# A spectral layer and a gated product on one core: the sequence transform split 64 x 32 instead of 32 x 64, real and imaginary parts stacked on partitions

## The chip, the cores and the metric

One core of one Trainium2 chip. The time is device microseconds (us) of one execution of the program, and "time" below is the median over executions; the profile is of one further execution. Engines are named as the profile names them: PE (TensorE; PEld are its weight loads), DVE (VectorE), ACT (ScalarE), POOL (GpSimd), SP (the queue that issues nearly all DMAs).

## What is computed

```python
def reference(A_x, A_w_r, A_w_i, B_x, B_w_gate, B_w_up, B_w_down):
    # x: [1, 2048, 640]; w_r, w_i: [2048, 321]; w_gate, w_up: [640, 1536]; w_down: [1536, 640]; all bf16
    xn = _layernorm(A_x, axis=-1)
    X = rfft2(xn, axes=(-2, -1))              # 2048 x 321, complex
    a = irfft2(X * (w_r + 1j * w_i), s=(2048, 640)).astype(bf16)
    b = ((xn @ w_gate) * (xn @ w_up)) @ w_down
    return A_x + a + b
```

## The kernel before

Rows of x are laid out as row = 16 p + j over 128 partitions p. After the layer norm the work has two branches that share every engine.

- The gated product: gate/up matmuls write PSUM (`GU`, narrow blocks of rows at L989, blocks of 512 rows at L969), `copy_on` evicts them (L719 when ACT does it, L720 when DVE does), `H` multiplies (L1005, L1006), and at the end 12 matmuls per output piece (`ACC`, L1229) sum over w_down; one more (`IV`, L1239) adds the spectral branch into the same bank, `FIN` (L1249) adds x and the piece is stored.
- The spectral branch: S1 to S5 (L883 to L917, DVE) do the small factors of the transform along the 640 columns; `R` (L930) the short part of the transform along the 2048 rows; then 16 steps t, each `D` (L1034, the 64-point part along columns), its eviction `eD`, `C` (L1055 to L1058, the long part along rows, a complex product with a real table), `WM` (L1070, L1073: the product with the filter w_r, w_i, four real products kept in fp32), `CD` (L1084, L1086, DVE) and `CB` (L1093, L1094, POOL), which combine the four products into a real and an imaginary part, `NG` (L1101 to L1103, ACT: negated or plain copies for the second operand), `IA` (L1117, L1118, the way back along rows) and its eviction `eIA`; then `I` (L1146) and V1 to V5 (L1170 to L1203, DVE).

The 2048 rows are split as 32 x 64 (`_R = 32`, `_S1 = 64`): R transforms over 32, C over 64, and one step holds one of 16 groups of 128 rows. The imaginary part lies beside the real one in the free dimension, so a complex product of C is four matmuls of 321 columns with three tables (cos, -sin, sin).

No loop order is written by hand. Every piece above is a task with the engines that may run it, a cost in ns (`_d_mm`, `_d_act`, ...), a priority and what it reads and writes. `_Sched.plan` plays the tasks through, choosing for each engine the task to start next, within `slack` of the most urgent one; `caps` bounds how many PSUM units a class of tasks may hold. The result is a fixed order of instructions on each engine, with semaphore waits between engines. A matmul task names a `bank`; the evicting task `frees` it.

Filters come by 64 DMAs (`ld_w`, L713), four a step, of 64 rows of 642 bytes each, into four slots; a slot is loaded again when the `WM` that read it is done. SP's queue is served in order, and it holds the loads of w_down too, which overwrite the inverse tables (`TI`) that IA reads.

The lines around C:

```python
a_r = v_a[:, ar, 0:_LP]
a_i = v_a[:, ar, 324:324 + _LP]
c.e.matmul(ps[:, bk, 0:_LP], v_tf[:, t, 0, :], a_r, start=True, stop=False)
c.e.matmul(ps[:, bk + 1, 0:_LP], v_tf[:, t, 0, :], a_i, start=True, stop=False)
c.e.matmul(ps[:, bk, 0:_LP], v_tf[:, t, 1, :], a_i, start=False, stop=True)
return c.e.matmul(ps[:, bk + 1, 0:_LP], v_tf[:, t, 2, :], a_r, start=False, stop=True)
```

Of the kernel before, what the change touches and what calls it, by code (L numbers as in the profile page):

```python
# [20 lines left out]
class _Task(object):  # L21
# [4 lines left out]
    def __init__(self, tid, name, engs, dur, emit, prio):  # L26
# [10 lines left out]
        self.frees = None  # L37
# [34 lines left out]
class _Sched(object):  # L72
# [55 lines left out]
    def task(self, name, engs, dur, emit, reads=(), writes=(), prio=0.0, after=(), bank=None, frees=None,  # L128
# [7 lines left out]
        t.frees = frees  # L136
        if selffree:
            t.freers.append(t)
        if frees is not None:
            frees.freers.append(t)  # L140
            t.deps.add(frees)
# [13 lines left out]
    def plan(self, nbanks=8, filler_deadline=0.0):  # L155
# [56 lines left out]
        while nsch < ntot:  # L212
# [107 lines left out]
            if t.frees is not None:  # L320
                p = t.frees
                pending_free[p.tid] -= 1
                fe = free_end.get(p.tid, 0.0)
                if t.end > fe:
                    free_end[p.tid] = t.end
                if pending_free[p.tid] == 0:
                    release(p)
# [58 lines left out]
_R = 32  # L386
_S1 = _S // _R
_RR = _S1 // 16
_G = 64 // _S1

# [8 lines left out]
def _build_tables():  # L399
# [56 lines left out]
    a = np.arange(16)[:, None, None, None]  # L456
    r = np.arange(_RR)[None, None, None, :]
    s1 = np.broadcast_to(a + 16 * r, (16, _G, 2, _RR)).reshape(128)
    mg = np.broadcast_to(np.arange(_G)[None, :, None, None], (16, _G, 2, _RR)).reshape(128)
    mck = np.broadcast_to(np.arange(2)[None, None, :, None], (16, _G, 2, _RR)).reshape(128)  # L460
    ng = np.repeat(np.arange(_G), 2 * _S1)
    npm = np.tile(np.repeat(np.arange(2), _S1), _G)
    nk1 = np.tile(np.arange(_S1), 2 * _G)
    tf = np.zeros((128, 16, 3, 128), np.float64)
    ti = np.zeros((128, 16, 2, 128), np.float64)
    for tt in range(16):
        k = _rows(tt, ng, npm, nk1)
        ph = two_pi * ((s1[:, None] * k[None, :]) % _S) / _S
        c = np.exp(-1j * ph)
        same = (mg[:, None] == ng[None, :]).astype(np.float64)  # L470
        ck = np.broadcast_to(mck[:, None], (128, 128))
        pm = np.broadcast_to(npm[None, :], (128, 128))
        f = np.where(ck == 1, np.where(pm == 1, -1j, 1j), 1.0 + 0j)
        i = f
        if tt == 0:
            own = (ck == pm).astype(np.float64)
            z0 = (ng[None, :] == 0)
            f = np.where(z0, own, f)
            i = np.where(z0, own, i)
        fm = c * f * same  # L480
        im = np.conj(c) * i * same / _S
        tf[:, tt, 0] = fm.real
        tf[:, tt, 1] = -fm.imag
        tf[:, tt, 2] = fm.imag
        ti[:, tt, 0] = im.real.T
        ti[:, tt, 1] = im.imag.T
# [5 lines left out]
def _rows(tt, g, pm, k1):  # L492
    q = tt * _G + g
# [15 lines left out]
_NW = 4  # L509
# [3 lines left out]
_YS = 1024  # L513
# [39 lines left out]
def _build(nc, A_x, A_w_r, A_w_i, B_w_gate, B_w_up, B_w_down, out, opts=None):  # L553
# [3 lines left out]
    with es:  # L557
# [8 lines left out]
        sch.caps = {"glu": opts.get("cap_glu", 2), "acc": opts.get("cap_acc", 4), "fill": 1}  # L566
        sch.caps["a"] = opts.get("cap_a", 2)
# [32 lines left out]
        b_w = alloc("W", _NW * 2 * 322)  # L600
        b_tf = alloc("TF", 16 * 3 * 128)
# [10 lines left out]
        b_p = alloc("P", 3 * 4 * 2 * _LP)  # L612
        b_y = alloc("Y", 2 * _YS)
        b_y3 = alloc("Y3", _YS, at=lay["STAT"][0])
# [24 lines left out]
        v_u = V("U").rearrange("p (j t a m) -> p j t a m", j=5, t=16, a=16)  # L639
# [3 lines left out]
        v_w = V("W").rearrange("p (r w l) -> p r w l", r=_NW, w=2)  # L643
# [4 lines left out]
        v_tf = V("TF").rearrange("p (t m k) -> p t m k", t=16, m=3)  # L648
        v_ti = V("TI").rearrange("p (t c n) -> p t c n", t=16, c=2)
# [14 lines left out]
        v_p = V("P").bitcast(_F32).rearrange("p (r w c l) -> p r w c l", r=3, w=2, c=2)  # L664
        v_y = [V("Y")[:, 0:_YS], V("Y")[:, _YS:2 * _YS], V("Y3")]
# [23 lines left out]
        b_wp = sch.buf("wp", 10 ** 9 + 500, 1)  # L689
# [35 lines left out]
        for q in range(4):  # L725
            dma("ld_tf%d" % q, v_tf[:, 4 * q:4 * q + 4], d_tf[:, 4 * q:4 * q + 4],
                128 * 4 * 768, [(b_tf, ("t", 4 * q, 4 * q + 4))], prio=0.31 + 0.01 * q)
# [4 lines left out]
        T("warm_zero", "dve", 150.0, em_wz, writes=[(b_dum, None)], prio=-1.0)  # L732
        for fi in range(opts.get("nfill", 70)):
            def em_fill(c):
                bk = bank_of(c.t)
                c.e.matmul(ps[:, bk, 0:128], v_dum[:, 0:128], v_dum[:, 128:256], start=True, stop=True)
                return c.e.matmul(ps[:, bk, 128:256], v_dum[:, 0:128], v_dum[:, 128:256], start=True,
                                  stop=True)
            T("fill%d" % fi, "pe", 2 * _d_mm(128), em_fill, prio=90.0 + 0.001 * fi, bank="single", cls="fill",
              selffree=True, reads=[(b_dum, None)])  # L740
        nwarm = opts.get("nwarm", 12)
# [8 lines left out]
        T("warm", "pe", opts.get("warm_ns", 5050.0), em_warm, reads=[(b_dum, None)], prio=-1.0,  # L750
          bank="pair", cls="warm", selffree=True)

        def em_wpad(c):
            return c.e.memset(v_w[:, :, :, 321:322], 0.0)
        wpad = T("w_pad", "dve", 80.0, em_wpad, writes=[(b_wp, None)], prio=3.0)


# [3 lines left out]
        muls = {}  # L761
        for gi, (b0, nb) in enumerate(_LN_GROUPS):
            pbase = 1.0 + 0.05 * gi if gi < 4 else opts.get("ln_prio", 5.99) + 0.05 * (gi - opts.get("ln_lead", 4))
            for b in range(b0, b0 + nb):
                if b >= opts.get("act_stats", 6):
# [577 lines left out]
```

## Time and profile before

| | |
|---|---|
| median of 13 runs | 207.05 us (206.52 to 208.01) |
| the profiled execution | 207.06 us, span of its instructions 205.3 us |
| granted TensorE clock | 1.00 |
| HBM read, written | 16.82 MB, 2.62 MB |
| instructions | 4513 |

In a line of groups the columns are: source line, engine, operation, output<-input with sizes, count; then busy us and mean ns of one; then idle time of the engine before them and what ended it. The mean of one is its length from start to end; successive ones overlap on every engine, so what one costs in a row is the distance from start to start, read from a stretch of several. In the chain of waits a line is start us, length us, and the engine (or DMA) and line that the end of the program was waiting for. In the stretches, "(x526)" is a count of instructions. A line of code that is a helper's (L719, L720, L713) gathers all that the helper did.

### The profile page before, as it was taken

The numbers are of one execution on the slowest core, as the hardware profiler recorded it, in microseconds if no ns is written. First come the engines' busy times: TensorE is split into PE (matmuls) and PEld (weight loads), VectorE is DVE, ScalarE is ACT, GpSimd is POOL, SyncE is SP. The second block draws the span as 40 slices with busy tenths as digits, with TensorE's granted clock in tenths as the row PEclk, the third lists the DMA queues.
The fourth block names the chain that finished last, engine by engine and source line by source line (L and its number), as shares of the span: only waits on it lengthen the run. The fifth ranks groups of instructions, "written<-read, shape, count | busy, mean of one in ns | idle before, by whom it ended". The sixth has DMA issues, their size and how long they took to land.

```text
span 205.3 us, 4513 instructions
## 1 busy us (share of the span) xinstructions
PE 200.9 (98%) x1695; PEld 136.9 (67%) x1695; DVE 179.2 (87%) x508; ACT 121.7 (59%) x282; POOL 21.6 (11%) x36
## 2 busy tenths in 40 slices
PE   7999999999999999999999999999999999999995
PEld 7997999554545455555776566656777787777774
DVE  3798999999999999859997897917999999999972
ACT  2388998999976577577999799887420221000000
POOL 0000000000000000004654266310000000000000
DMA  6999990703139360001232343125033122323212
GB/s 187 298 341 381 392 202 7 67 0 64 32 66 248 79 200 0 3 0 31 54 66 65 79 104 69 60 64 160 3 96 113 51 80 83 112 79 110 82 37 63
DMA packets 30740, 21.69 MB, mean 106 GB/s; under 512 B 10752, under 2 KB 29696, under 8 KB 30592
## 3 DMA queue, kind: packets, MB, share of 16 engines
q1 hardware_dynamic: 29920, 21.06, 39.7%
q10 hardware_dynamic: 800, 0.36, 0.6%
q8 instruction: 13, 0.21, 0.5%
q14 instruction: 7, 0.06, 0.1%
HBM read 16.82 MB, written 2.62 MB: 95 GB/s over the span
## 4 chain that ended last, share of the span: by engine, by line
PE 81%; SPq 6%; DMA 5%; DVE 5%; ACT 1%; issue 1%
PE ps L969 34%; PE ps L1229 25%; PE ps L989 9%; SPq L713 6%; DMA arena<-in_A_x_dram 4%; DVE arena L1070 2%; PE ps L930 2%; PE ps L1146 2%; PE ps L1239 2%; PE ps L1034 1%; DMA arena<-in_A_w_i_dram 1%; PE ps L1117 1%; PE ps L1118 1%; DVE arena L1073 1%; DVE arena L1005 1%; PE ps L1055 1%
## 5 line engine op out<-in xcount | busy, mean ns | idle before, releaser
L719 ACT ACTIVATE arena<-ps 128x512 bf16<-128x512 f32 (+5 forms) x183 | 97.2, 568 | 48.8 <-PE ps L1146 23.4
L969 PE MATMUL ps<-arena 128*128 128x512 bf16 x360 | 82.3, 379 | 0.4 <-DVE arena L1073 0.4
L969 PEld LDWEIGHTS ps<-arena 128*128 128x128 bf16 x360 | 33.9, 98 | 36.9 <-ACT arena L719 0.8
L1229 PE MATMUL ps<-arena 128*128 128x320 bf16 (+2 forms) x396 | 56.7, 295 | 0.0
L1229 PEld LDWEIGHTS ps<-arena 128*128 128x128 bf16 x396 | 38.0, 98 | 13.9
L989 PE MATMUL ps<-arena 128*128 128x128 bf16 (+1 forms) x360 | 28.4, 237 | 0.4 <-ACT arena L719 0.2
L989 PEld LDWEIGHTS ps<-arena 128*128 128x128 bf16 x360 | 24.9, 98 | 2.9 <-ACT arena L719 1.3
L1005 DVE TENSOR_TENSOR arena<-arena 128x512 bf16<-128x512 bf16 x36 | 15.8, 439 | 9.3 <-ACT arena L719 9.0
L1070 DVE TENSOR_TENSOR arena<-ps,arena 128x256 f32<-128x256 f32 x64 | 22.6, 418 | 1.4 <-PE ps L1058 1.2
L1093 POOL TENSOR_TENSOR arena<-arena 128x256 bf16<-128x256 f32 x16 | 10.3, 645 | 112.6 <-DVE arena L1086 112.6
L1249 DVE TENSOR_TENSOR arena<-ps,arena 128x320 bf16<-128x320 f32 (+2 forms) x33 | 15.4, 477 | 3.8 <-PE ps L1239 3.8
L1094 POOL TENSOR_TENSOR arena<-arena 128x256 bf16<-128x256 f32 x16 | 11.7, 733 | 0.0
L1118 PE MATMUL ps<-arena 128*128 128x128 bf16 x80 | 10.4, 219 | 0.0
L1117 PE MATMUL ps<-arena 128*128 128x128 bf16 x80 | 10.4, 219 | 0.0
L1117 PEld LDWEIGHTS ps<-arena 128*128 128x128 bf16 x80 | 8.7, 111 | 1.8 <-issue 0.3
L1118 PEld LDWEIGHTS ps<-arena 128*128 128x128 bf16 x80 | 8.7, 112 | 1.3
L1239 PE MATMUL ps<-arena 128*128 128x320 bf16 (+2 forms) x33 | 9.1, 295 | 0.0
L883 DVE TENSOR_TENSOR arena<-arena 128x384 f32<-128x384 bf16 x16 | 8.9, 554 | 0.0
L782 DVE BATCH_NORM_STATS2 arena<-arena 128x6 f32<-128x320 bf16 x12 | 5.5, 482 | 3.3 <-DMA arena<-in_A_x_dram 3.1
L773 ACT ACTIVATE arena<-arena 128x640 bf16<-128x640 bf16 x10 | 8.2, 824 | 0.0
L767 ACT ACTIVATE arena<-arena 128x640 bf16<-128x640 bf16 x10 | 7.3, 732 | 0.7 <-DMA arena<-in_A_x_dram 0.6
L1073 DVE TENSOR_TENSOR arena<-ps,arena 128x260 f32<-128x260 f32 x16 | 7.1, 441 | 0.0
(72 smaller groups left out, 236.4 us busy)
## 6 DMA issues: line engine op xcount, KB each, us to landing
arena<-in_A_x_dram SPq DMA_DIRECT2D x20, 160.0 KB, 2.5
out_dram<-arena SPq DMA_DIRECT2D x31, 80.0 KB, 1.6
arena<-c_tf SPq DMA_DIRECT2D x4, 384.0 KB, 10.9
arena<-in_A_w_r_dram SPq DMA_DIRECT2D x32, 40.1 KB, 2.3
arena<-in_A_w_i_dram SPq DMA_DIRECT2D x32, 40.1 KB, 2.3
arena<-in_B_w_gate_dram SPq DMA_DIRECT2D x4, 320.0 KB, 5.4
arena<-in_A_x_dram SPq DMA_DIRECT2D x1, 1280.0 KB, 9.9
arena<-c_ti SPq DMA_DIRECT2D x2, 512.0 KB, 5.0
```

The lines of the kernel that those rows point to most:

```text
L713: return c.e.dma_start(dst, src)
L719: return c.e.activation(dst, src, _ACTF.Copy)
L969: ins = c.e.matmul(ps[:, bk, :], v_gw[:, w, j, ft, :], v_xt[:, j, rows], start=(j == 0), stop=(j == 4))
L989: ins = c.e.matmul(ps[:, bk, w * n:(w + 1) * n], v_gw[:, w, j, ft, :], v_xt[:, j, rows], start=(j == 0), stop=(j == 4))
L1005: return c.e.tensor_tensor(v_ht[:, ft0, rows], v_gbf[:, rr, 0, :], v_gbf[:, rr, 1, :], _OP.mult)
L1070: c.e.tensor_tensor(v_p[:, ar, w, :, 128 * h:128 * h + 128].rearrange("p c (m k) -> p c m k", k=4), xh.rearrange("p c (m k) -> p c m k", k ...
L1094: return c.e.tensor_tensor(v_y[ar][:, 256:512], p00[:, 0:256], p11[:, 0:256], _OP.subtract)
L1117: c.e.matmul(dst, l1, v_ti[:, t, 0, :], start=True, stop=False)
L1118: ins = c.e.matmul(dst, l2, v_ti[:, t, 1, :], start=False, stop=True)
L1229: ins = c.e.matmul(ps[:, bk, 0:sl3.stop - sl3.start], v_ht[:, ft, a * 128:(a + 1) * 128], v_wd[:, ft, sl3], start=(ft == 7 and px is None) ...
L1239: return c.e.matmul(ps[:, bank_of(own), 0:sl3.stop - sl3.start], v_sm[:, 2, :], v_v[:, a, sl3], start=False, stop=True)
L1249: return c.e.tensor_tensor(v_out[:, a % 2, sl3], ps[:, bk, 0:sl3.stop - sl3.start], v_xr[:, xs, sl3], _OP.add)
```

## The change

The rows are split 64 x 32 (`_R = 64`, `_S1 = 32`). A step now holds two of 32 groups q (`_G = 2`), each with 64 rows; real and imaginary parts of these 64 lie interleaved on the 128 partitions. Sixteen steps remain.

- D computes real and imaginary halves by separate matmuls of 64 or 65 columns (ten a step instead of five). eD becomes two tasks of two copies of 64 partitions x 321, which move halves between partitions 0 to 63 and 64 to 127.
- C is one matmul a group with one table that holds the complex product: two a step instead of four.
- WM writes the bf16 products with w_r and w_i directly to where IA reads them; CD and CB are gone. IA's table does the combination: its weights are the products, its moving operand has 64 columns, and there are 20 matmuls a step instead of 10. NG negates 2 x 256 elements on ACT or DVE, the new NS copies or negates 3 small pieces on POOL.
- Each filter row is now needed on two partitions; the loads are per two steps, with four rows in a run outermost, 50 DMAs in place of 64, in two slots; 5.3 MB instead of 2.6 MB land.
- Tables for C shrink from 1.5 to 1.0 MB. The warm-up has 40 matmuls instead of 48, fillers wait for the first transpose, block 1 of the layer norm takes its statistics on ACT, and caps, slacks and priorities of the planner are others, so the order of instructions changes on every engine.

```diff
-_R = 32
+_R = 64
 _S1 = _S // _R
 _RR = _S1 // 16
 _G = 64 // _S1
+_NQ = 16 * _G
...
+        tf[0:64, q, n_re] = fm.real
+        tf[0:64, q, n_im] = fm.imag
+        tf[64:128, q, n_re] = -fm.imag
+        tf[64:128, q, n_im] = fm.real
+        ti[n_re, q, 0] = im.real
+        ti[n_im, q, 0] = -im.imag
+        ti[n_re, q, 1] = im.imag
+        ti[n_im, q, 1] = im.real
...
-_NW = 4
+_NW = 2
+_WQ = 4
...
-        sch.caps = {"glu": opts.get("cap_glu", 2), "acc": opts.get("cap_acc", 4), "fill": 1}
-        sch.caps["a"] = opts.get("cap_a", 2)
+        sch.caps = {"glu": opts.get("cap_glu", 4), "acc": opts.get("cap_acc", 4), "fill": 1}
+        sch.caps["glu2"] = opts.get("cap_glu2", 2)
+        sch.caps["a"] = opts.get("cap_a", 3)
...
-        nwarm = opts.get("nwarm", 12)
+        nwarm = opts.get("nwarm", 10)
...
+        aset = set(opts.get("act_set", (1,))) | set(range(opts.get("act_stats", 6), 16))
...
-            pf = opts.get("f_prio", 6.05) + 0.05 * g
+            pf = opts.get("f_prio", 5.8) + 0.05 * g
...
-        c_at = [6.3 + opts.get("c_rate", 1.8) * (b0 + nb - 1) for b0, nb in _CHUNKS]
+        c_at = [6.3 + opts.get("c_rate", 2.2) * (b0 + nb - 1) for b0, nb in _CHUNKS]
...
-            for w_ in range(2):
-                for h in range(2):
-                    k2 = int(_rows(t, 0, h, 0))
-                    dma("ld_w%d_%d_%d" % (t, w_, h), v_w[64 * h:64 * h + 64, wr, w_, 0:321], wvs[w_][:, k2, :],
+            wr = (t // (_WQ // 2)) % _NW
+            if t % (_WQ // 2) == 0:
+                q0 = 2 * t
+                for w_ in range(2):
+                    wv, dw = wvs[w_], v_w[:, wr, w_]
+                    parts = [(dw[0:64], wv[:, q0:q0 + _WQ, :].rearrange("k1 q l -> k1 (q l)").unsqueeze(1).to_broadcast(
+                        [_S1, 2, _WQ * 321]), 64 * _WQ * 642)]
...
+                    for d_ in range(2):
+                        parts.append((dw[64 + d_:128:2, 321 * o_:321 * _WQ].rearrange("p (q l) -> p q l", l=321),
+                                      wv[:, _R - q0 - o_:_R - q0 - _WQ:-1, :], 32 * (_WQ - o_) * 642))
...
                 for k in range(5):
-                    n = 128 if k < 4 else 130
+                    n = 64 if k < 4 else 65
+                    for w in range(2):
+                        ins = c.e.matmul(ps[:, bk + w, k * 64:k * 64 + n], v_uq[:, k, t, :],
+                                         v_fd[:, k * 128 + w * n: k * 128 + w * n + n], start=True, stop=True)
...
+            for w in range(2):
+                def em_ed(c, td=td, ar=ar, w=w):
...
+                    for g in range(2):
+                        ins = copy_on(c, v_a[64 * w:64 * w + 64, ar, 324 * g:324 * g + 321],
+                                      ps[64 * g:64 * g + 64, bk, 0:321])
+                eds.append(T("eD_%d_%d" % (t, w), ("act", "dve"), {"dve": 1000.0, "act": 880.0},
...
+                for g in range(2):
+                    ins = c.e.matmul(ps[:, bk + g, 0:_LP], v_tf[:, 2 * t + g, :], v_a[:, ar, 324 * g:324 * g + _LP],
+                                     start=True, stop=True)
...
+                for g in range(2):
...
+                    for h in range(2):
+                        xh = ps[:, bk + g, 0:256].rearrange("p (k h m) -> p h m k", k=4, h=2)[:, h]
...
+                        c.e.tensor_tensor(dst, xh.unsqueeze(1).to_broadcast([128, 2, 32, 4]), wv, _OP.mult)
+                    x5 = ps[:, bk + g, 256:321].unsqueeze(1).to_broadcast([128, 2, 65])
+                    ins = c.e.tensor_tensor(d5, x5, wg[:, :, 0:321:5], _OP.mult)
...
-            T("CB_%d" % t, ce, {"dve": 2 * _d_dve(256), "pool": opts.get("cb_pool", 1430.0)}, em_cb,
...
+                if c.e is nc.scalar:
+                    return c.e.activation(yg[:, :, 0:256], yg[:, :, 512:768], _ACTF.Copy, scale=-1.0)
+                return c.e.tensor_scalar(yg[:, :, 0:256], yg[:, :, 512:768], -1.0, None, _OP.mult)
...
+                c.e.tensor_copy(yg[:, :, 833:896], yg[:, :, 1025:1088])
+                c.e.tensor_scalar(yg[:, :, 896:961], yg[:, :, 1024:1089], -1.0, None, _OP.mult)
+                return c.e.tensor_copy(yg[:, :, 961:1024], yg[:, :, 769:832])
+            T("NS_%d" % t, opts.get("ns_eng", ('pool',)), {"act": 3 * _d_act(128), "pool": 1200.0, "dve": 420.0}, em_ns,
...
-                    dst = psflat[:, bk * 512 + k * 128: bk * 512 + (k + 1) * 128]
-                    c.e.matmul(dst, l1, v_ti[:, t, 0, :], start=True, stop=False)
-                    ins = c.e.matmul(dst, l2, v_ti[:, t, 1, :], start=False, stop=True)
+                        dst = psflat[:, bk * 512 + k * 128: bk * 512 + (k + 1) * 128].rearrange(
+                            "p (a g m) -> p g a m", a=16, g=2)[:, g]
+                        c.e.matmul(dst, l1, v_ti[:, 2 * t + g, 0, :], start=True, stop=False)
+                        ins = c.e.matmul(dst, l2, v_ti[:, 2 * t + g, 1, :], start=False, stop=True)
...
-            pa = 19.0 + opts.get("i_rate", 0.2) * a
+            pa = 19.0 + opts.get("i_rate", 0.05) * a
...
-                       prio=opts.get("iv_prio", 30.0) + 0.05 * a + 0.01 + 0.001 * hf, after=[ag2])
+                       prio=opts.get("iv_prio", 19.0) + 0.05 * a + 0.01 + 0.001 * hf, after=[ag2])
...
-                       prio=opts.get("fin_prio", 5.0) + 0.05 * a - 0.001, frees=own, after=[iv])
+                       prio=opts.get("fin_prio", 30.0) + 0.05 * a - 0.001, frees=own, after=[iv])
...
-        sch.slack["act"] = opts.get("slack_act", 500.0)
-        sch.slack["dve"] = opts.get("slack_dve", 600.0)
+        sch.slack["act"] = opts.get("slack_act", 700.0)
+        sch.slack["dve"] = opts.get("slack_dve", 800.0)
```

## The prediction

> **What bounds the kernel now.** I read the page's busy shares first, then the chain of waits in order of time, then the busy time of each engine in three stretches.
>
> ```profile
> PE 200.9 (98%) x1695; PEld 136.9 (67%) x1695; DVE 179.2 (87%) x508; ACT 121.7 (59%) x282; POOL 21.6 (11%) x36
> ```
> ```profile
> 8.83 7.93 DMA arena<-in_A_x_dram
> 16.79 0.83 ACT arena L767 x2
> 17.62 0.49 ACT arena L719
> 18.15 1.27 PE ps L989 x10
> ...
> 54.91 10.79 PE ps L969 x50
> ...
> 86.81 0.56 PE ps L930 x10
> ...
> 91.44 0.14 PE ps L1055
> ...
> 143.63 1.63 PE ps L1229 x12
> ```
> ```profile
> 18.15:89.36 71.21, 71.18 (x526) 42.59 (x526) 67.71 (x196) 57.06 (x123) 0.00 (x0) 1.00 0.48 112
> 89.36:136.60 47.24, 46.67 (x409) 30.31 (x408) 38.88 (x128) 41.85 (x114) 21.37 (x32) 1.00 0.26 58
> 136.60:203.00 66.40, 66.36 (x542) 48.27 (x539) 59.62 (x141) 13.15 (x22) 0.00 (x0) 1.00 0.29 85
> ```
>
> The rows of the last fence give stretch, length, then the busy us of PE, PEld, DVE, ACT, POOL. From 18.15 us TensorE does not pause: D of step 0 starts at 89.36, IA of step 15 ends at 136.6, the rest are the final sums. So what TensorE no longer issues shortens the time, unless it then waits. The chain also gives the pitches, length over count: 56 ns for 128 columns (0.56/10), 137 for 321 (0.14 each), 136 for 320 (1.63/12), 216 for 512 (10.79/50).
>
> **TensorE's own work.** C falls from 64 to 32 matmuls of 321 columns: 32 x 0.137 = 4.4 us less. D goes from 80 of 128 or 130 columns (4.5 us) to 160 of 64 or 65; IA from 160 of 128 (8.9 us) to 320 of 64. No row is narrower than 128. The line through 512 and 128 columns, (216 - 56)/384 = 0.417 ns a column, gives 56 - 64 x 0.417 = 29 ns at 64: the low end. The high end is the nearest row as it stands, 56 ns, were it the weight load that sets it. Against that speak two loads after a pause:
>
> ```profile
> 112.11 0.10 PEld L1055 LDWEIGHTS ps<-arena 128*128 128x128 bf16 x1 [0.50 <-DMA arena<-in_A_w_i_dram]
> 112.12 0.10 PEld L1056 LDWEIGHTS ps<-arena 128*128 128x128 bf16 x1
> ```
> ```profile
> L1117 PEld LDWEIGHTS ps<-arena 128*128 128x128 bf16 x80 | 8.7, 111 | 1.8 <-issue 0.3
> ```
>
> They begin 0.01 to 0.02 us apart, so a load does not occupy the array's loading path for 56 ns. IA's loads, which read every fourth element, take 111 ns where the others take 98; 13 ns on some 15 is about 28, still at the low end. I take 29 ns for D (4.7 us) and 31 for IA (9.9 us). Net: -4.4 + 0.2 + 1.0 = -3.2 us; by the ends -3.8 and +8.9.
>
> [...]
>
> **The start.** The warm-up has 40 instead of 48 matmuls, but TensorE's start into its unbroken run is set elsewhere: rows 4 to 7 of x land at 16.79, and ScalarE's queue has their statistics (L767) ahead of the evictions that free TensorE's banks. The loads up to there are the same in the same order. In the changed program's order 13 narrow evictions precede that wait, not 12, so 10 more gate/up matmuls are done (0.56 us), and the eviction behind it has 256 columns instead of 512 (0.38 and 0.58 us long, 0.2 less). Together -0.8; ends 0 and -1.5, the pause before 18.15 in which no matmul is issued (the 40 from 14.45 at 56 ns are out by 16.7).
>
> **Up to the last R.** 190 wide gate/up matmuls precede the last R (L930), not 215: TensorE gets there 25 x 0.216 = 5.4 us sooner, at 86.64 - 0.8 - 5.4 = 80.4. Its input, the last L917, ended at 86.2 on a VectorE that was busy 67.7 of 71.2 us. Counted in the new order at the pitches of the old rows, VectorE has 61.3 us of work between the landing at 16.79 and that point, where it had 65.2 (four normalizations now on ScalarE, three H products and a first S2 elsewhere, an eviction less). So it ends at 82.3 if its waits stay, 80.5 if its 1.8 us of waits there go. R is late by 0 to 2; I take 0.9.
>
> **The spectral stage, D to IA.** Here 150 wide gate/up matmuls lie, where there were 115; TensorE's part is 150 x 0.216 + 4.7 + 4.4 + 9.9 = 51.4 us (47.0 before). VectorE's, at old pitches: 64 filter products x 0.331, 32 of 130 elements x 0.20 (between the 0.136 of 65 and 0.345 of 260), 16 of the 64 eD pieces x 0.40 (that of L1249, 320 wide), 18 H x 0.335, 8 NG x 0.28 (L819, 640 wide, has 0.296), 7 evictions 4.8: 47.4 us, where 38.9 were busy. ScalarE: 48 eD pieces x 0.32, 28 x 0.48, 14 x 0.58, 8 NG x 0.52 and one last eviction: 41.5, as before. Twice the eD pieces thus lie beside TensorE's filler, and cost nothing while VectorE keeps about 4 us free. If that cover goes, WM is late, then NG and NS, then IA.
>
> GpSimd gets three pieces of 126 to 130 elements a step. Its rows are 0.10 us (a memset of one element) and 0.65 to 0.73 (256 elements, two inputs): 0.3 to 2.1 us a step; I take 1.0. The shortest cover between a C and its IA in the new order is IA, three D, gate/up, C, gate/up: 0.62 + 0.87 + 1.08 + 0.27 + 1.08 = 3.9 us, against WM 1.7, NS 1.0 and 0.4 of hops: covered. At 2.1 it would be 0.3 late in four places.
>
> Filter loads: two slots of two steps, 6 issues a group instead of 4 a step.
>
> ```profile
> L713 SPq DMA_DIRECT2D arena<-in_A_w_i_dram x32: 582/597/1637, 64.8 to 126.1; - x32
> DMA to landing us min/median/max: 1.5/2.3/11.3
> ```
>
> With 0.64 us from issue to issue, a group has landed 5 x 0.64 + 2.3 = 5.5 us after WM frees the slot. VectorE's work until the next user is 7.9, 7.9, 5.2, 7.1, 5.2, 7.1 us for groups 2 to 7; ahead of group 4 in SP's queue stands a down-weight load that waits for IA 4 (0.6). Late by 0.9 and 0.3; part is hidden by TensorE's cover: 0.7, in place of the 0.5 us wait at 112. The low end is 0. Were an issue as dear as the w_up load issued at 4.91 (1.04), a group would take 7.7 us, and VectorE would stand 6.8 us in all.
>
> GpSimd and VectorE can also hold each other up:
>
> ```profile
> 114.83 0.74 POOL L1094 TENSOR_TENSOR arena<-arena 128x256 bf16<-128x256 f32 x1
> 114.86 0.99 DVE L1005 TENSOR_TENSOR arena<-arena 128x512 bf16<-128x512 bf16 x1 [0.70 <-ACT arena L719]
> ```
>
> H took 0.99 us instead of 0.42, ending 0.28 after GpSimd's end: one hit in 36. I keep it at nothing more. [...]
>
> **Sum**, against the profiled execution's span: 205.3 - 3.2 - 0.8 + 0.9 + 0.2 = 202.4. That execution took 207.06 (median of the runs 207.05), 1.76 around its span: **204.2 us**. The last stage keeps its work: 33 sums on TensorE, 56.8 to 56.4 us on VectorE.
>
> **Rivals.** (1) Narrow matmuls stay at 56 ns: 160 x 27 + 320 x 25 ns = 12.3 us more, 216.5. For it: no narrower row exists. Against: the loads 15 ns apart. (2) The slower side that I fear most: VectorE becomes the bound between D and IA. From L917's end at about 81.9 it has 47.4 us of work and whatever it waits, and TensorE needs its last NG at about 135 (IA 15 would end at 136.6 - 0.8 - 3.2 + 0.9 + 0.2 + 10 x 0.216 = 135.9). It decides once VectorE's waits there pass 6 us. Before, it had 6.5 between 86.2 and 128.3. [...] For it: 92% load, one queue in order. Against: TensorE's old pauses were only about 1.2 us there, and the planner's costs for eD (1.0 and 0.88 us a pair) are above the rows' 0.8 and 0.64, so that the real order runs ahead of the planned one. (3) Dear filter issues: 6.8 us on VectorE in place of 1.2, of which 5 reach the end: 209. [...] That C is not halved can be ruled out from the instruction order.
>
> **How the numbers follow.** Forecast 0.66, its own range 201.8 to 206.3; rival 2 0.14; rival 1 0.06; rival 3 0.06; rival 4 0.08, mostly inside 0.2% of 207.05, which is about what a measurement here can tell from none. The range for 8 in 10 runs from 201.5 to 208.5: it leaves out rival 1, rival 3 and part of 2. Faster 0.68 (the forecast and a little of rival 4), same 0.06 (the rest of it), slower 0.26 (rivals 1 to 3).
>
> **What would show it.** IA's matmuls 29 to 32 ns apart, D's 29; the unbroken run starting near 17.9 with 10 more gate/up matmuls behind it; the last R at 81 to 82, waiting for VectorE; IA 15 ending near 136; filter waits only ahead of WM 8 and 12. Wrong if the pitch is near 56, or if TensorE pauses over 3 us between D and IA.

## The result: slower by 0.7%

| | before | after |
|---|---|---|
| median of the runs, us | 206.78 (48 runs, 206.16 to 208.01) | 208.25 (11 runs, 207.45 to 209.21) |
| profiled execution, span, us | 205.3 | 206.8 |
| its last narrow gate/up matmul starts | 37.34 | 38.20 |
| D of step 0 starts | 89.36 | 84.83 |
| IA of step 15, last matmul starts | 137.42 | 141.15 |
| first final sum (ACC) starts | 143.47 | 144.45 |

The ratio after to before is 1.0066, with a 95% interval of 1.0051 to 1.0081. The forecast was 204.2 us, with a gain: the sign was wrong. The profiled execution of after took 208.91 us, 0.66 above its median; why is a point below.

The busy shares of after, and its three stretches in the view by windows (stretch, length, then the busy us of PE, PEld, DVE, ACT, POOL):

```profile
PE 200.1 (97%) x1917; PEld 136.2 (66%) x1917; DVE 182.3 (88%) x513; ACT 128.3 (62%) x263; POOL 18.9 (9%) x52
```
```profile
18.15:84.83 66.68, 66.47 (x495) 40.75 (x493) 64.29 (x192) 57.13 (x123) 0.00 (x0) 1.00 0.50 121
84.83:141.21 56.38, 54.16 (x664) 33.71 (x663) 48.05 (x140) 49.28 (x97) 18.71 (x48) 1.00 0.35 90
141.21:205.00 63.79, 63.30 (x524) 46.60 (x520) 58.67 (x140) 11.59 (x19) 0.00 (x0) 1.00 0.29 84
```

The middle stretch, D of step 0 to IA of step 15, is where TensorE now stands still: 54.16 busy of 56.38 us, where the stretch of before had 46.67 of 47.24 (to 136.60, 0.8 us ahead of IA's last matmul). ScalarE is busy 49.28 us in it; the prediction had 41.5. The chain of waits of after in that stretch (start, us, what) names what TensorE waits for:

```profile
96.93 0.71 ACT arena L714
97.69 0.47 PE ps L1050 x10
98.17 2.33 PE ps L973 x10
...
112.41 0.70 issue
113.11 0.43 PE ps L1073 x2
114.25 0.71 ACT arena L714
115.01 0.47 PE ps L1050 x10
...
118.88 0.29 issue
119.17 0.43 PE ps L1073 x2
...
125.83 0.28 issue
126.11 0.43 PE ps L1073 x2
127.24 0.71 ACT arena L714
128.00 0.47 PE ps L1050 x10
...
131.86 0.30 issue
132.16 0.43 PE ps L1073 x2
```

These are three kinds of pauses. The start-to-start times of TensorE's instructions give them as 4.1 us in all, 1.1 in before (the busy time shows less, as it counts each matmul to its end, which in after lies 0.20 us behind its start at 64 columns and 0.38 at 512):

- The third D (L1050) of three triples waits 0.37 us for the 0.71 us copy of an IA result (L714, 128x640), which frees the PSUM banks that this D takes; the gate/up group behind it waits another 0.16 to 0.19 us for WM's last instruction (L1094), for a bank as well: 1.6 us.
- C8 at 113.11 and C12 at 126.11 wait 0.86 and 0.44 us for the last of their group's filter loads, landed at 113.02 and 126.02. C itself waits, not only WM: `hold(tc, wm)` gives C the things that WM waits for. The page calls these pauses "issue" because the last load landed on a semaphore that several loads share.
- C9, C10, C13 and C14 wait 0.12, 0.45, 0.09 and 0.46 us for a copy of the D result (L714, 64x321): 1.1 us. The view calls the pauses ahead of C10 and C14 "issue" too; the copies end at 119.07 and 132.06, 0.10 us before these C start.

### The profile page after: what moved, and what is told of

Same layout as the page of the kernel before. It is cut to its first block, busy times and chain, and to the rows that moved or that the text cites. A ratio compares the mean times of both kernels' runs of the same rounds, so it can differ in the third digit from the quotient of the medians.

```text
span 206.8 us, 4949 instructions
## 1 busy us (share of the span) xinstructions
PE 200.1 (97%) x1917; PEld 136.2 (66%) x1917; DVE 182.3 (88%) x513; ACT 128.3 (62%) x263; POOL 18.9 (9%) x52
## 4 chain that ended last, share of the span: by engine, by line
PE 83%; DVE 7%; DMA 3%; SPq 3%; ACT 2%; issue 1%
PE ps L973 38%; PE ps L1245 25%; PE ps L993 4%; DMA arena<-in_A_x_dram 3%; SPq L708 3%; PE ps L1134 3%; PE ps L1133 3%; PE ps L1073 3%; PE ps L934 2%; PE ps L1162 2%; PE ps L1255 2%; PE ps L1050 2%; ACT arena L714 1%; DVE arena L1010 1%; DVE arena L887 1%
## 5 line engine op out<-in xcount | busy, mean ns | idle before, releaser
L714 ACT ACTIVATE arena<-ps 128x512 bf16<-128x512 f32 (+5 forms) x196 | 103.4, 556 | 41.7 <-PE ps L1162 23.1
L973 PEld LDWEIGHTS ps<-arena 128*128 128x128 bf16 x360 | 33.9, 98 | 36.1 <-ACT arena L714 1.5
L1245 PEld LDWEIGHTS ps<-arena 128*128 128x128 bf16 x396 | 37.9, 98 | 13.7
L993 PEld LDWEIGHTS ps<-arena 128*128 128x128 bf16 x360 | 25.1, 98 | 2.8 <-issue 0.4
L1091 DVE TENSOR_TENSOR arena<-ps,arena 128x256 bf16<-128x256 f32 x64 | 24.0, 417 | 1.1 <-PE ps L1073 1.0
L715 DVE CAST arena<-ps 64x321 bf16<-64x321 f32 (+3 forms) x26 | 14.7, 564 | 3.4 <-PE ps L1050 1.3
L1115 POOL COPY arena<-arena 128x126 bf16<-128x126 bf16 x16 | 6.6, 411 | 119.9 <-DVE arena L1094 119.9
L1133 PEld LDWEIGHTS ps<-arena 128*128 128x128 bf16 x160 | 12.1, 116 | 1.9 <-issue 0.4
L1134 PE MATMUL ps<-arena 128*128 128x64 bf16 x160 | 12.8, 198 | 0.0
L1133 PE MATMUL ps<-arena 128*128 128x64 bf16 x160 | 12.8, 197 | 0.0
L1134 PEld LDWEIGHTS ps<-arena 128*128 128x128 bf16 x160 | 11.3, 115 | 1.3
L1094 DVE TENSOR_TENSOR arena<-ps,arena 128x130 bf16<-128x130 f32 x32 | 9.4, 295 | 0.0
L772 ACT ACTIVATE arena<-arena 128x640 bf16<-128x640 bf16 x11 | 9.1, 825 | 0.1
L781 DVE BATCH_NORM_STATS2 arena<-arena 128x6 f32<-128x320 bf16 x10 | 4.7, 483 | 4.8 <-DMA arena<-in_A_x_dram 4.8
L1116 POOL TENSOR_SCALAR arena<-arena 128x130 bf16<-128x130 bf16 x16 | 8.7, 542 | 0.0
```

Source lines behind the costliest of these rows:

```text
L714: return c.e.activation(dst, src, _ACTF.Copy)
L715: return c.e.tensor_copy(dst, src)
L973: ins = c.e.matmul(ps[:, bk, :], v_gw[:, w, j, ft, :], v_xt[:, j, rows], start=(j == 0), stop=(j == 4))
L993: ins = c.e.matmul(ps[:, bk, w * n:(w + 1) * n], v_gw[:, w, j, ft, :], v_xt[:, j, rows], start=(j == 0), stop=(j == 4))
L1091: c.e.tensor_tensor(dst, xh.unsqueeze(1).to_broadcast([128, 2, 32, 4]), wv, _OP.mult)
L1133: c.e.matmul(dst, l1, v_ti[:, 2 * t + g, 0, :], start=True, stop=False)
```

## The experiments

Every ratio is to the kernel before, run on the same chip at the same time; after itself is at 1.0066. By the intervals a difference of two ratios is good to some 0.0025, or 0.5 us. Line numbers are those of after. "Order unchanged" means that every queue issues the same tasks in the same sequence as after; where an edit would have made the planner choose another one, the sequence was fixed from after's plan.

| run | edit | ratio | 95% interval |
|---|---|---|---|
| e1_whole | D copied by 128x321 copies | 0.9990 | 0.9972 to 1.0008 |
| e2_slot3 | third filter slot | 1.0045 | 1.0027 to 1.0064 |
| e3_contig | IA's weights contiguous | 1.0059 | 1.0033 to 1.0086 |
| e4_front | start of the kernel before | 1.0269 | 1.0241 to 1.0298 |
| e5_wdmove | one load moved on SP | 1.0054 | 1.0034 to 1.0074 |
| e6_half | straight 64x321 copies | 1.0033 | 1.0017 to 1.0049 |
| e7_sum | e1, e3 and e5 together | 0.9938 | 0.9919 to 0.9957 |
| e8_replan | planner told measured costs, two settings | 0.9901 | 0.9883 to 0.9920 |
| e9_settings | e8's settings, not its costs | 1.0240 | 1.0214 to 1.0265 |
| e10_before_best | best order found for before | 0.9971 | 0.9956 to 0.9986 |
| e11_slots | e2 and e5 together | 1.0010 | 0.9991 to 1.0028 |
| e12_before_again | before, a second profile | 1.0005 | 0.9990 to 1.0021 |
| e13_same | 64x321 copies, same start partition | 1.0008 | 0.9991 to 1.0025 |
| e14_replan_whole | e8 with 128x321 copies | 0.9892 | 0.9866 to 0.9918 |

### The copies of the D result: e1, e6, e13

```diff
-                    for g in range(2):
-                        ins = copy_on(c, v_a[64 * w:64 * w + 64, ar, 324 * g:324 * g + 321],
-                                      ps[64 * g:64 * g + 64, bk, 0:321])
+                    ins = copy_on(c, v_a[:, ar, 324 * w:324 * w + 321], ps[:, bk, 0:321])
```

> The changed kernel with each pair of 64-partition copies of the D result (64x321, two per task) made one straight 128x321 copy; every queue keeps the changed kernel's order. The swap of halves between partitions is left out, so the output is not the reference's. Theory eD: in the trace of after the third D of three triples waits 0.37 us for an ACT copy, C10 and C14 0.45 us each, C9 and C13 0.1 us each, about 2.2 us in all, because a pair of pieces takes 0.89 us (ACT) or 1.00 us (VectorE). With one copy of some 0.4 us these pauses go and the time falls by 1.5 to 2.3 us: 206.0 to 206.8, ratio to before 0.996 to 1.000. Rival (the loss is in the front and in the 33 ns pitch of IA, and the pauses only move to the next wait, WM or the filters): the time falls by less than 0.6 us, ratio 1.004 or more, and the pauses of C8 and C12 grow.

The time fell by 0.0076 of 207, 1.6 us. C9, C10, C13 and C14 no longer wait for a copy, and C12's pause is 0.16 us instead of 0.44. The three pauses of the third D stayed at 0.37: the expectation had put them down to the same copies, and they wait for the copy of IA. C8's pause stayed at 0.86.

```diff
-                        ins = copy_on(c, v_a[64 * w:64 * w + 64, ar, 324 * g:324 * g + 321],
+                        ins = copy_on(c, v_a[64 * g:64 * g + 64, ar, 324 * w:324 * w + 321],
                                       ps[64 * g:64 * g + 64, bk, 0:321])
```

> The changed kernel with the same two 64-partition copies per task of the D result, each now straight (partitions 0 to 63 to 0 to 63, 64 to 127 to 64 to 127) instead of crossing halves; order of every queue unchanged. The output is not the reference's, the swap of halves is left out. Straight 128x321 copies followed one another on ACT every 0.318 us in e1_whole; crossing 64x321 pieces every 0.445 us. If it is the crossing between halves that keeps a copy from overlapping the one before, the pitch of the straight pieces is 0.32 to 0.36 us and the time falls by 0.6 to 1.0 us. If it is the 64 partitions, or that two copies read one bank, it stays at 0.43 to 0.45 us and the time stays within 0.4 us of after's.

In a pair, the second copy still came 0.43 to 0.45 us after the first, so it is not the crossing that holds it. Yet the time fell by 0.0033 of 207, 0.7 us (0.2 to 1.1 by the intervals), where that rival allows 0.4. The trace offers a reason: in after, the first copy of the tasks with w = 1, which reads partitions 0 to 63 and writes 64 to 127, began 25 ns after a 512- or 640-wide copy had ended (six times); straight, it begins 103 to 113 ns before that end.

```diff
                         ins = copy_on(c, v_a[64 * w:64 * w + 64, ar, 324 * g:324 * g + 321],
-                                      ps[64 * g:64 * g + 64, bk, 0:321])
+                                      ps[64 * w:64 * w + 64, bk, 0:321])
```

> The changed kernel with the second 64x321 copy of each task reading the same half of the partitions as the first and as its output, so that both copies of a task start at the same partitions; still 64 partitions each, order of every queue unchanged. One half of each D result is copied twice and the other left out, so the output is not the reference's. In e6_half straight pieces, too, followed each other only after the end of the one before (gap +12 ns), but there the second piece starts at partition 64 and the first at 0; in e1_whole 128-partition copies, all from partition 0, overlapped by 0.1 us. [...] Rival (64 partitions as such): the pitch in a pair stays at 0.43 to 0.45 us and the time within 0.4 us of after's.

Still 64 partitions, so these as such do not set the pitch: now the second copy of a pair comes 0.318 to 0.339 us after the first on ScalarE, 0.40 to 0.42 on VectorE (after: 0.432 to 0.448, 0.49 to 0.50); the time fell by 0.0058 of 207, 1.2 us, and C10 and C14 no longer pause, while C12 pauses 0.76 us (0.44 in after). One row of the timeline shows it in each trace, a 128x512 copy and the copies of D that follow it without a pause, four in after and in e13_same, two in e1_whole (start, us from the first start to the last end):

```profile
85.03 2.28 ACT L714 ACTIVATE arena<-ps 128x512 bf16<-128x512 f32 x5 [0.48 <-PE ps L973]
```
```profile
84.12 1.89 ACT L714 ACTIVATE arena<-ps 128x512 bf16<-128x512 f32 x5 [0.48 <-PE ps L973]
```
```profile
84.10 1.26 ACT L714 ACTIVATE arena<-ps 128x512 bf16<-128x512 f32 x3 [0.48 <-PE ps L973]
```

2.28 us in after, 1.89 in e13_same, 1.26 in e1_whole. The groups by shape do not show it, because they give the length of one instruction and not the distance to the next. Here they are for after, e6_half and e1_whole:

```profile
L714 ACT ACTIVATE arena<-ps 64x321 bf16<-64x321 f32 x48 | 20.9, 435 | 0.7
```
```profile
L714 ACT ACTIVATE arena<-ps 64x321 bf16<-64x321 f32 x48 | 20.8, 433 | 0.5
```
```profile
L714 ACT ACTIVATE arena<-ps 128x321 bf16<-128x321 f32 x24 | 9.5, 444 | 0.0
```

433 to 444 ns each, whatever the height. What differs is whether the next one begins 0.1 us before that end or 0.01 to 0.03 after it, and one description fits all of these copies and their successors in the three traces: a copy whose input or output starts at another partition (0 or 64 here) than the previous instruction's begins only when that one has ended.

### The filter loads: e2, e5, e11

e2 adds a slot, in a buffer of its own, which the lines below leave out; e5 moves the load of the first down-projection slices behind the filter loads in SP's sequence; e11 does both.

```diff
-_NW = 2
+_NW = 3
```

> The changed kernel with a third slot for the filters; every queue keeps the changed kernel's order, tile for tile, so only the loads start earlier. Theory filters: C8 and C12, which wait 0.86 and 0.44 us for a filter load in the trace of after, no longer wait; the time falls by 0.9 to 1.3 us, ratio to before 1.000 to 1.002. Rival (the loads are a cover: behind them the same steps wait for the copies of D or for WM): the two pauses go and others of the same size appear within the next 5 us, the time falls by less than 0.4 us, ratio 1.004 or more.

C8 still waited 1.00 us: the extra slot stood free, but SP did not get to its loads. C12 no longer waited, and C14's pause fell from 0.46 to 0.13 us, but the gate/up group behind the third D after C12 now waited some 0.6 us instead of 0.19 for WM (L1094); the time fell by 0.4 us, no more than its interval.

```diff
 # SP's sequence
-... ld_wd0, ld_w8_0_0 to ld_w14_1_2, ld_wd2, ...
+... ld_w8_0_0 to ld_w14_1_2, ld_wd0, ld_wd2, ...
```

> The changed kernel, every queue in the changed kernel's order, but on SP the load of the first two down-projection slices (2 x 160 KB) stands behind the filter loads instead of ahead of group 4's. In the trace of after and of e2_slot3 that load goes out at 106.22 and 105.84 us, when IA4 has released the table that it overwrites, and group 4's six filter loads only behind it, at 106.67 to 109.93, although the third slot of e2_slot3 was free from the start. Theory SP order: group 4's loads go out when WM3 has ended (its slot's last reader), before 103 us, C8 no longer waits for them (0.86 us before), and C10, which waited 0.45 us for copies that C8's pause had delayed, waits less; the time falls by 0.7 to 1.3 us, ratio to before 1.000 to 1.003. Rival: the order of SP is no cause either, the loads wait for WM5 itself; C8 keeps a pause over 0.5 us and the time stays within 0.4 us of after's.

The expectation named the wrong last reader: a group serves two steps, so the slot's is WM5, as the rival says. C8's pause fell from 0.86 to 0.46 us, the time by no more than its interval.

> The changed kernel with both of e2_slot3's and e5_wdmove's edits: a third filter slot, and the down-projection load behind the filter loads on SP; all else in the changed kernel's order. e5_wdmove showed that group 4's loads, freed of that load, still wait for WM5, the last reader of their slot (issues 105.79 to 108.96, last landing 111.77, C8 0.46 us late). Theory (slot and order both held the loads): now they go out before 104 us, C8 and C12 wait for no filter load, and 0.7 to 1.0 us go, if the copies do not take the wait over: ratio 1.001 to 1.004. Rival (behind the filters stand the copies of D and the banks, as e3_contig, where IA got shorter and the pauses grew, suggests): the filter waits vanish, the pauses of C10 and C14 and of the third D stay, and the time is within 0.3 us of e5_wdmove's, ratio 1.004 to 1.007.

The time fell by 0.0056 of 207, 1.2 us, where the theory had 0.7 to 1.0. C8 and C12 no longer pause. C10 and C14 pause 0.12 and 0.14 us, where the rival had them stay at 0.45: they had been late because C8 and C12 were, and in e2, where C12 alone was freed, C14 alone recovered. The banks took some of it back: the gate/up groups behind two of the three third D wait some 0.6 us for WM instead of 0.16 and 0.19. The loads of group 4 in SP's timeline, of after, e5_wdmove and e11_slots in turn:

```profile
106.22 0.39 SPq L708 DMA_DIRECT2D arena<-in_B_w_down_dram  x1
106.67 1.93 SPq L708 DMA_DIRECT2D arena<-in_A_w_r_dram  x3
108.64 1.89 SPq L708 DMA_DIRECT2D arena<-in_A_w_i_dram  x3
```
```profile
105.79 1.84 SPq L708 DMA_DIRECT2D arena<-in_A_w_r_dram  x3
107.67 1.89 SPq L708 DMA_DIRECT2D arena<-in_A_w_i_dram  x3
```
```profile
97.16 1.83 SPq L708 DMA_DIRECT2D arena<-in_A_w_r_dram  x3
99.03 1.89 SPq L708 DMA_DIRECT2D arena<-in_A_w_i_dram  x3
```

The move alone brings them 0.9 us forward, the two edits together 9.5, and only then does C8 find its filters landed; for C12 the slot alone had been enough. For C8 these are two holds in series: taking away one shows next to nothing.

### IA's weights: e3, and the three parts together: e7

```diff
-                            l1, l2 = yg[:, 256 + k:768:4], yg[:, k:512:4]
+                            l1, l2 = yg[:, 256 + 128 * k:384 + 128 * k], yg[:, 128 * k:128 + 128 * k]
```

> The changed kernel with the 256 weights of IA that are read with a stride of 4 elements read contiguously instead; every queue keeps the changed kernel's order. The products go to IA in another order of elements, so the output is not the reference's. Theory pitch: IA's matmuls, 33 to 34 ns apart in the trace of after, come 29 ns apart as D's do, and 256 x 4.5 ns = 1.2 us of TensorE time go; IA is not waited for by itself, so the time falls by 0.8 to 1.2 us, ratio 1.001 to 1.003. Rival (D to IA is paced by ACT and VectorE, not by TensorE's sum): the pauses grow by what IA gives up, the time falls by less than 0.4 us, ratio 1.005 or more. If the pitch stays at 33 ns, the stride is not the cause.

IA's weight loads, in after and in e3_contig:

```profile
L1133 PEld LDWEIGHTS ps<-arena 128*128 128x128 bf16 x160 | 12.1, 116 | 1.9 <-issue 0.4
```
```profile
L1133 PEld LDWEIGHTS ps<-arena 128*128 128x128 bf16 x160 | 10.6, 98 | 1.9 <-issue 0.4
```

98 ns instead of 116 on average (a fifth of these loads was contiguous before, too), and the matmuls come 29 ns apart instead of 33 to 34: the stride is the cause of the pitch. The time fell by 0.0007, nothing that can be measured, since C8 now waits 1.27 us (0.86 in after), C10 0.53, C12 0.64 and C14 0.53. What IA gives up, the pauses take.

> e1_whole, e3_contig and e5_wdmove in one kernel, order of every queue as in the changed kernel but for the one load. The swap of halves is left out and IA gets its products in another order, so the output is not the reference's. Theory (several waits that stand behind one another, each hiding the next): together they give more than apart, the pauses of C8 to C14 go, and the time falls by the 1.4 us of the copies, 1.0 to 1.2 us of IA's pitch and 0.5 to 1.0 us of the load: 204.5 to 205.5, ratio 0.988 to 0.994, the gain that the prediction had looked for. Rival (PSUM banks: the three pauses of 0.37 us of the third D and 0.2 us behind WM stay and others come): 206 or more, ratio 0.996 or more.

0.0128 of 207, 2.6 us less than after, where the three alone took off 1.6, 0.1 and 0.25; that they give more together than apart is not shown, since 0.6 us lies within the intervals. The time is the theory's, but not all of its pauses went: the third D's stay, as the rival has it, and with two slots C8, C12 and C14 still wait 0.78, 0.42 and 0.28 us.

### The start: e4, e12

The edits in short:

```diff
-aset = set(opts.get("act_set", (1,))) | ...
+aset = set(opts.get("act_set", ())) | ...
-nwarm 10, warm_ns 4280.0, fills of 4 x 64 columns, tied to T0_0
+nwarm 12, warm_ns 5050.0, fills of 2 x 128 columns, not tied
-(part, "dve") if part == "act" else part
+part
```

> The changed kernel with the start of the kernel before: block 1's statistics on VectorE again, 48 warm-up matmuls, fillers 128 wide and not tied to the first transposes, the first eviction's small part on ACT alone; the planner's priorities stay the changed ones, and the order of the gate/up units after it comes out otherwise. Theory front: the last narrow gate/up pair starts at 37.3 to 37.6 us rather than 38.2, and up to 0.9 us of the loss goes. Rival (the start is set by the landing of the x rows: blocks 1, 2 and 3 landed 0.6, 0.5 and 1.6 us later in the profiled execution of after than in that of before, with the same loads issued by then): the last narrow pair stays at 38.0 to 38.5 unless the loads of this run land early, and the time changes by less than 0.4 us either way from this.

The last narrow matmul started at 37.16 (the expectations call it the last narrow pair), but the plan that followed was another and the whole took 212.6 us. So it tells of the start only that, and not what the start is worth.

> The kernel before, unchanged, for a second profile of its start and as a control. In eight profiles the last narrow gate/up pair starts at 37.1 to 38.2 us, late where the rows of block 3 land late (37.3 with 11.6 to 11.9, 37.8 with 12.8, 38.2 with 13.2 and 12.4). Theory (the late start of the profiled execution of after is that landing, which varies from run to run): here the last narrow pair starts at 37.2 to 38.0, following the landing in the same way. Rival (the changed start loses 0.9 us by itself): 37.3 to 37.4 whatever the landing. Ratio 0.998 to 1.002.

37.38 in this profile of before, its rows of block 3 landed at 11.64. In the nine profiles that have after's start, the last narrow matmul started six times at 37.1 to 37.3 (rows landed at 11.7 to 12.1) and three times late: 37.82 (12.81), 38.16 (12.36, a gate/up load late too) and 38.20, in after (13.18). The chain of waits of after shows that landing:

```profile
6.58 6.61 DMA arena<-in_A_x_dram
...
13.21 0.89 DVE arena L781 x2
```

So the 0.9 us that the profiled execution of after loses at the start against before goes with that execution's landing. The changed start is worth about nothing, neither the gain forecast nor a loss. Why these rows land late in one execution and not in another was not tried.

### The order: e8, e9, e10, e14

The edits of e8 in short (e9 has the last pair of lines alone):

```diff
-            ia = T("IA_%d" % t, "pe", 20 * _d_mm(64), ...
+            ia = T("IA_%d" % t, "pe", 20 * 33.5, ...
-            return T(name, q, _DMA_ISSUE, em, ...          (500 ns)
+            return T(name, q, iss, em, ...                 (645 ns for filters and down-projection)
-slack_dve 800.0, c_rate 2.2
+slack_dve 400.0, c_rate 2.0
```

> The changed kernel, complete, with a new order of the queues: the planner is told the measured 33.5 ns for a matmul of IA (29.2 before) and 645 ns for an issue of a filter or down-projection load (500 before), and two of its settings differ (VectorE's slack 400 instead of 800, rate of the gate/up units 2.0 instead of 2.2). Theory (the parts gain, the order lost it): without the pauses ahead of C8 to C14 the time is 204.6 to 206.3, ratio 0.989 to 0.997. Rival (the parts themselves lose: copies in quarters, IA's pitch): 207.3 or more, ratio 1.001 or more.

204.63 us (204.48 to 204.88): the change with all its parts, and 1% faster than before. Its middle stretch has no pause:

```profile
81.25:136.71 55.46, 55.46 (x679) 34.87 (x678) 48.46 (x142) 49.55 (x100) 19.01 (x48) 1.00 0.35 91
```

ScalarE is as busy as in after (49.55 us), the copies as dear, IA's pitch as long.

> The changed kernel, complete, with the two settings of e8_replan (VectorE's slack 400, rate of the gate/up units 2.0) but with the costs that the planner was told in the change (29.2 ns for a matmul of IA, 500 ns for an issue). Theory (e8_replan's gain is that of an order planned on the durations the chip has): this order, planned on the wrong ones, is worse than e8_replan's by 3 us or more, 207.5 or more, ratio to before 1.003 or more. Rival (the two settings alone are better, whatever the costs): within 1 us of e8_replan's 204.6, ratio below 0.995.

> The kernel before, complete, with five settings of its planner changed (slack of TensorE 2000 for 1500 and of VectorE 800 for 600, affinity 450 for 300, rate of the gate/up units 2.6 for 1.8, priority of S1 to R 5.6 for 6.05), the best order that a search over the same settings found for it. Theory (e8_replan is faster because of the change's parts, its order only lets them through): the kernel before has little left in its order, 206.0 to 207.0, ratio 0.996 to 1.000. Rival (a search over orders gives any kernel that much): 205.3 or less, ratio below 0.993.

211.6 and 205.9 us. The planner puts a start and an end to every task. Beside the traces its figures tell which plans held (us; the planned end includes the last store):

```
                  planned end   measured median   difference
before               206.8          206.8            0.0
after                205.8          208.25          +2.5
e4_front             210.9          212.6           +1.7
e9_settings          208.5          211.6           +3.1
e8_replan            204.9          204.6           -0.2
e10_before_best      206.4          205.9           -0.5

start in the trace less planned start
            D_0     C_8    GU_4_12_0   C_10    C_12    C_14    I_0
before    -1.27   -1.81     -1.48     -1.49   -1.17   -1.20   -1.20
after     -0.50   +0.65     +0.06     +0.72   +1.30   +1.36   +1.53
e8_replan -1.76   -1.92     -1.92     -1.94   -1.97   -2.00   -2.08
```

(The row of after starts 0.9 too high for the late landing.) After's plan was better than before's by 1.1 us and came out 2.5 late: it had given IA's matmuls 29.2 ns and the loads' issues 500, and it was tight, so that each IA took 0.09 us longer and C8, C10, C12 and C14 each lost 0.44 to 0.86 us. Played through with 33.5 and 645 ns instead, after's own order ends at 207.3 in the planner's reckoning, so these two costs account for some 1.6 of the 2.5 us; what makes up the rest was not found.

The three plans made on the change's costs came out 1.7 to 3.1 us late; e8's, made on measured ones, did not. Two of the three also ran with a slowed TensorE: its granted clock was 0.50 for 6.8 us from 141 in e4_front and for 3.4 us from 104 in e9_settings (means of the two profiled executions 0.984 and 0.992), each time just after waits of more than 2 us within 4, and IA's matmuls came 53 ns apart there; after and e8_replan had 1.00 throughout. So their lateness is not the costs' alone. And e9_settings does not isolate the costs: its order was worse than e8's by 3.6 us already in the plan. It shows that the two settings alone do not do it. The costs alone do not either: with e8's costs and one of its two settings put back, the planner's own end is 207.9 or 210.8 instead of 204.9, so that e8 is also one good draw out of a search. For before the same search finds 0.4 us, and 0.6 were measured. With the best order found for each, the change is worth 0.9901 / 0.9971 = 0.993, some 1.4 us (0.9 to 1.9 by the intervals).

> e8_replan with the two 64-partition copies per task made one straight 128x321 copy, as in e1_whole, every queue in e8_replan's order; the swap of halves is left out, so the output is not the reference's. Theory (in e8_replan's order the copies lie beside gate/up work and hold nothing up): the time stays within 0.3 us of e8_replan's 204.6, ratio 0.988 to 0.992, although ScalarE loses over 10 us of work. Rival (the copies still cost in any order): 0.8 us or more less, ratio 0.986 or less.

The ratio is 0.0009, or 0.2 us, lower, which is within the intervals, with 13 us less work on ScalarE in that stretch (36.43 busy, 49.55 in e8_replan):

```profile
81.25:136.71 55.46, 55.46 (x677) 34.87 (x676) 46.41 (x138) 36.43 (x72) 18.68 (x48) 1.00 0.35 91
```

In this order the copies are covered. In after's they cost 1.6 us.

## Why the prediction was wrong

The sum was 205.3 - 3.2 - 0.8 + 0.9 + 0.2 = 202.4 us of span. Measured was 206.8, term by term:

| step of the prediction | forecast | measured | off by |
|---|---|---|---|
| TensorE's own work (C, D, IA) | -3.2 | -2.4: C 137 ns and D 29 as forecast, IA 33 to 34 instead of 31 | +0.8 |
| the start | -0.8 | -0.1 in six of nine profiles, +0.9 in the profiled execution | +0.7, and +0.9 for the late landing (that execution's bad luck) |
| the last R late for VectorE | +0.9 | 0: at 82.11 in after, its input done at 81.33 | -0.9 |
| pauses between D and IA | 1.3 in all (filters 0.7, the rest of before's) | 4.1 | +2.85 |

202.4 + 0.8 + 0.7 + 0.9 - 0.9 + 2.85 = 206.75. The third row is an error the other way that hid 0.9 us of the miss. Two of the prediction's readings were off besides, without weight: IA of step 15 in before ends 0.8 us or more behind the 136.6 given, and its terms for VectorE add up to 47.1 and not 47.4.

**The step that failed** is the spectral stage: "Twice the eD pieces thus lie beside TensorE's filler, and cost nothing while VectorE keeps about 4 us free." Both halves were wrong. The pieces were costed at 0.32 and 0.40 us, from rows of copies that all start at partition 0; they take 0.445 and 0.50, which is the planner's 0.88 and 1.0 a pair within 0.01. The text named that difference and decided against the planner ("so that the real order runs ahead of the planned one"), when the rows it held against it were of another kind. And to cost nothing while an engine has time free is an argument from sums. VectorE did keep its time free (48.05 busy of 56.38 us), and ScalarE too (49.28), and still C10 and C14 stood behind one copy each: the order decides, not the load. With whole copies in the same order 1.6 us went (e1_whole), with halves that keep their start partition 1.2 (e13_same).

**Filters** were the right mechanism with the right places (C8 and C12, the down-projection load ahead of group 4), and were mis-sized: 0.7 us forecast, 1.3 in the trace and 1.2 in e11_slots (a group had landed 2.7 to 3.8 us after its last issue, where the sum took 2.3). That TensorE itself stands, since C waits for what WM waits for, was not seen.

**The PSUM banks** had no term at all: 1.6 us for the third D and the gate/up group behind it, in an order that stacks IA, C and three D into eight banks. No run took this wait away by itself, so its price is read from the trace and not shown by an experiment; in e8_replan's order it does not occur.

**The start**: "the 40 from 14.45 at 56 ns are out by 16.7" took all of the matmuls ahead of the long wait for 128 columns wide. Half were 256 wide, so the pause that the ten extra gate/up matmuls were to fill was some 0.4 us and not 1.5. The first transpose (T0_0) does start 0.6 us earlier, but in eight of the nine profiles TensorE then stands 0.4 to 0.8 us at about 9 (in after for a w_up load).

**The rivals**: VectorE as the bound (chance 0.14) has the sign and not the mechanism. Narrow matmuls stayed far from 56 ns: D's came 29 apart and IA's 33 to 34, 29 with contiguous weights (e3_contig). No H or NG was held up by GpSimd for long: the longest H took 0.51 us, where before had one of 0.99.

## What to carry to other kernels

Where a planner fixes the order, its costs are part of the kernel: compare its planned starts with the trace, task by task, and where the difference jumps there is the wait, and often a cost that it was not told. A copy that is cheap by the length of its row may still be dear by its distance to the next (here 0.435 us long, and the next 0.32 to 0.34 or 0.43 to 0.46 us after its start): read start to start, and look at the partition where it starts. And take two suspected holds away together before calling either harmless.

## What the runs showed of the hardware

- On ScalarE, a 64x321 copy from PSUM lasts 0.435 us, like a 128x321 one (0.444). Behind a copy with the same start partitions it begins 0.1 us before that one's end (pitch 0.32 to 0.34 us, e13_same), behind one with another start partition of input or output (0 against 64) 0.01 to 0.03 us after it (0.43 to 0.46, after). On VectorE the pitches are 0.40 to 0.42 (e13_same) and 0.49 to 0.53 us (after).
- Weights of which four fifths are read at a stride of four elements: 116 ns a load on average instead of 98, matmuls of 64 columns 33 to 34 ns apart instead of 29 (after, e3_contig).
- A filter group of 657 KB, in six DMAs issued 0.64 us apart, had landed 2.7 to 3.8 us after the start of its last issue (after).
- Behind waits of TensorE of more than 2 us within 4, its granted clock stood at 0.50 for 3.4 us (e9_settings) and 6.8 us (e4_front).
